# Two feed-forward networks behind a block-causal attention: one run for the eight wide down pieces of a step, another last visit, and an order for the scores

## The chip, the cores and the metric

One core of a Trainium2 chip runs the kernel. The metric is the device time of one execution in microseconds (us). A matmul runs on TensorE and writes PSUM; VectorE, ScalarE and GpSimd work elementwise beside it, GpSimd on SBUF alone; DMA queues are issued from SyncE (SP) and ScalarE.

## The reference

Attention over 4 batches of 8 heads, 576 positions and 64 values a head, then two feed-forward networks without a residual, on 2304 tokens of 512 values with 2048 hidden values:

```python
scores = q @ k.T / sqrt(64)                 # masked to block_i >= block_j, blocks of 64
attn = softmax(scores)                      # with 1e-9 in the denominator
x = (attn @ v)                              # to 2304 tokens x 512
h = x @ moe_w_in;  x = (h * sigmoid(h)) @ moe_w_out
h = x @ moe2_w_in; x = (h * sigmoid(1.702 * h)) @ moe2_w_out
```

## The kernel before

**Planning.** The kernel doesn't issue instructions in the order of its text. Each operation is handed to `Flow.add` (line 45) with its engine, an estimated duration, what it reads and writes, and a due time `at`. `Flow.run` (line 89) then simulates the engines: whenever one is free it issues the ready operation with the smallest due time. The order on each engine's queue is what comes out of this. The planner knows PSUM by banks; the waits that the program really gets are made from tiles. Banks 0 and 1 are one tile, `s8` (shown as `s` in the trace), the others have one each.

**Attention** works on 16 pairs of heads. Scores of a pair are 9 bands of rows (`AT`, line 456, says in which bank each lies), computed in three parts, `s_mm` 0, 1 and 2 (line 475 in the trace): part 0 holds bands 6, 7 and the tail of 8, part 1 holds 8, 5 and 1, part 2 the four small ones. Bands 8 and 6 lie in `s8`. `s_max` takes the row maxima on VectorE (line 485), `s_exp` the exponentials on ScalarE (line 495), `t_mm` transposes (line 549), `t_cp` copies them to SBUF (lines 408, 409), `o_mm` multiplies by the values (line 593) and `x_out` writes into `xy`, which holds all tokens. `plan` gives each of these a due time, `p * TAU + when`, and `HEAD` replaces it for the first two pairs.

**The networks** use a fast matrix scheme: a token block of 768 columns (`W`) is cut into two halves of 384, and seven up products (lines 724 to 726, six matmuls of 384 columns each, 128-row operands split into a high and a low part) give a pair of hidden blocks. `keep` (line 733) copies products 1 and 2 out of PSUM on ScalarE as c11 and c22, `comb` (line 738) adds the others on VectorE, and `hidden` (lines 752 to 754) makes the activation in two parts: two activations on ScalarE and a subtraction on VectorE. Products alternate between the two banks of `UB`. Hidden blocks live in three buffers, `g0` to `g2`. The down projection (lines 791 to 793) of a hidden block is cut into pieces (i, m, big): i is which of the two hidden blocks, m which 128 output rows, and big says whether it is the first 512 columns of the token block, or the last 256. A piece is three matmuls.

**Steps and visits.** A visit (l, z, p0, p1) takes token block z of layer l through weight pairs p0 to p1; its results add up in PSUM. A step is one pair: its seven up products, and between them the 16 down pieces of the step before. `SEQ` (line 843) is the pattern (M an up product, D a piece), `ORDER` (line 841) the order of the pieces, `LAST` that of the pieces behind the last step; a chain of edges keeps TensorE in this order. There are 48 steps. At a visit's end `evac` (line 805) copies PSUM out: a whole visit (`"all"`) straight to `xy`; a visit of half the pairs puts its part into DRAM (`"first"`), and `"last"` fetches it again and adds. The weights are brought from 64-bit data to two 32-bit parts by `w_scale` to `w_put` on ScalarE, VectorE and GpSimd, spread by the strings `SUM_ON` to `Y_ON` (p GpSimd, d VectorE), with earliest times in `EARLY`.

Of the kernel before, what the change touches and what calls it, by code (L numbers as in the profile page):

```python
# [134 lines left out]
def act(n):  # L135
    return 0.06 + n * 0.833e-3


def dve(n):
    return 0.06 + n / 960  # L140
# [18 lines left out]
def block_causal_attention_two_ffn(  # L159
# [9 lines left out]
    nc = tc.nc  # L169
    PSUM = bass.MemoryType.PSUM  # L170

    NP, P, S = qT.shape
    BLK = 64
# [7 lines left out]
    H = 256  # L181
    A, B = slice(0, BLK), slice(BLK, P)
# [7 lines left out]
    NWF = 8  # L190
    NSR = 6
    DIRECT = "1e11111100010101"
    VISITS = [(0, 0, 0, 4), (0, 1, 0, 8), (0, 2, 0, 8), (0, 0, 4, 8), (1, 1, 0, 4), (1, 2, 0, 8), (1, 0, 0, 8), (1, 1, 4, 8)]
    EARLY = [6.4, 47.4, 34.1, 18.5, 68.3, 94.6, 93.9, 120.4, 40.0, 36.9, 88.0, 0.0]
    SUM_ON = "dpdddppdpddddpdppdddppdpdpddddddppddppddddpdpppddppddppppdppppdp"
    COMB_ON = "ppdpddpddddpddddddddpddpddppddppddppppdpdddddpppdpdpdddppdppppdd"
    LOW_ON = "pppdpdddpddpdpdpdpddpddddpdpdpdddddpddpdddpdddddppdpdpdpdppppdppppdpppdpddpdpppddpddppdpppdpppddppdddpdppddppddpdppdpppdpppdpdpdppddpddddppdddpp"
    X_ON = "pdddpppp"
    Y_ON = "pppdppdddppppp"
    NWARM = 3  # L200
    TAU = 66.730
    LEADS = [90.0, 82.0, 24.0, 80.0]
    BEFORE = 1e4

# [1 line left out]
    add = flow.add  # L206
# [21 lines left out]
    bank = {i: T("psum", [P, 512], F32, f"bank{i}") for i in range(2, 8)}  # L228
# [4 lines left out]
    xy = T("cst", [P, ND, NT], F32, "xy")  # L233
# [4 lines left out]
    def xkeys(m, c0, n):  # L238
        return [("xy", m, i) for i in range(c0 // H, (c0 + n - 1) // H + 1)]
# [151 lines left out]
    def op(eng, us, fn, reads=(), writes=(), lag=0.0, size=0, sb=False, mode=0):  # L391
        x = add(eng, us, fn, reads, writes, clock[0] - BEFORE, lag=lag, size=size, name=tag[0], sb=sb, mode=mode)
        for k in [*reads, *writes]:
            ends["a2" if k[0] in ("q", "k", "pj") else "a3"].append(x)
        return x
# [54 lines left out]
    PIECES = [[0], [0, 1], [1]]  # L450
# [5 lines left out]
    def swapped(j):  # L456
        return j in SIDES[1]
# [8 lines left out]
    def s_mm(p, part):  # L466
        (q, kq), (k, kk) = src(p, "q"), src(p, "k")
        keys = sorted({("B", AT[j][0] + (AT[j][1] + c) // 512) for _, *blocks in ROUNDS[part] for j, c in blocks})

        def mms():  # L470
            for n, *blocks in ROUNDS[part]:
                for j, c in blocks:
                    for h, r in enumerate((A, B)):
                        t = s_out(j)[B if h != swapped(j) else A, c:c + n]
                        nc.tensor.matmul(t, q[r, j * BLK:(j + 1) * BLK], k[r, c:c + n], start=True, stop=True)  # L475

        us = sum(max(n * 4 / 2400, 0.117) for n, *_ in ROUNDS[part]) + 0.02
        op("pe", us, mms, [(*kq, i) for i in PIECES[part]] + [kk], keys, lag=0.25, mode=1)

    def mx_(p, j):  # L480
        return buf(p, f"mx{j}", [P, 1])

    def s_max(p, *js):
        for j in js:
            op("dve", dve((j + 1) * BLK) + 0.01, lambda j=j: nc.vector.tensor_reduce(  # L485
                out=mx_(p, j), in_=s_view(j), axis=AX.X, op=ALU.max, negate=True), s_keys(j) + [kpj(p, 6)] * (j == 8), [("mx", p % 2, j)])

    exps = {}
# [110 lines left out]
    def x_out(p, odd):  # L599
# [5 lines left out]


    plan = [
        (0, 2882.13, load, "q"), (0, 2559.47, load, "k"), (0, 2853.51, load, "v"), (0, 2905.64, q_scale),
        (0, 2571.85, s_mm, 0), (0, 2852.24, s_max, 6), (0, 2571.21, s_max, 7), (0, 2553.46, s_exp, 6), (0, 2574.72, s_exp, 7),
        (0, 2909.22, s_mm, 1), (0, 2548.52, s_max, 8), (0, 2859.72, s_max, 5, 1), (0, 2571.07, s_exp, 8), (0, 2571.14, s_exp, 5, 1),  # L610
        (1, 2528.21, r_add), (1, 2578.60, r_inv),
        (1, 2548.41, t_mm, 4), (1, 2546.87, t_cp, 4, "act"), (1, 2539.51, t_mm, 5), (1, 2953.00, t_cp, 5, "dve"), (1, 2543.63, t_mm, 2), (1, 2880.99, t_cp, 2, "act"),
        (1, 2573.39, t_mm, 6), (1, 2559.80, r_copy, "act"), (1, 2951.06, t_cp, 6, "dve"), (1, 2571.01, r_put), (1, 2848.29, r_get),
        (0, 2528.64, s_mm, 2), (0, 2853.46, s_max, 3, 2), (0, 2550.49, s_max, 4, 0), (0, 2543.88, s_exp, 3, 2), (0, 2544.58, s_exp, 4, 0),
        (0, 2864.95, t_mm, 3), (0, 2674.64, t_cp, 3, "act"), (0, 2560.07, t_mm, 0), (0, 2823.46, t_cp, 0, "act"), (0, 2537.30, t_mm, 1), (0, 2541.48, t_cp, 1, "dve"),
        (1, 2859.78, o_mm, 0), (1, 2906.59, x_out, 0), (1, 2541.65, o_mm, 1), (1, 2542.10, x_out, 1),
    ]
    HEAD = [
        [1331.35, 1183.59, 1237.43, 1178.46, 1181.21, 1177.07, 1237.42, 1338.75, 1233.62, 1208.86, 1178.82, 1171.94, 1336.59, 1186.67, 1185.06, 1336.24, 1194.98, 1335.90, 1324.40, 1175.47, 1181.33, 1218.37, 1322.23, 1167.71, 1186.69, 1323.52, 1218.49, 1181.33, 1325.54, 1178.91, 1324.53, 1196.09, 1175.99, 1323.28, 1327.08, 1198.04, 1194.56, 1189.76, 1217.91, 1179.86, 1175.67, 1188.66],
        [1225.77, 1102.38, 1243.55, 1132.89, 1117.25, 1261.59, 1247.55, 1083.79, 1246.56, 1245.30, 1264.82, 1261.35, 1250.56, 1160.55, 1223.04, 1245.52, 1201.93, 1121.74, 1217.49, 1248.42, 1264.66, 1239.58, 1158.04, 1143.68, 1217.77, 1152.81, 1245.54, 1151.65, 1132.78, 1267.65, 1245.33, 1142.47, 1064.30, 1245.04, 1241.74, 1148.17, 1130.98, 1249.77, 1102.40, 1135.54, 1251.23, 1201.93],  # L620
    ]

    def attention():
# [177 lines left out]
    def evac(l, z, m, big, part, t):  # L801
        c0 = z * W + (0 if big else 2 * H)
        t -= LEADS[3]
        if big:
            src, dst, keys, bk = bank[YB[m]], xy[:, m, c0:c0 + 2 * H], xkeys(m, c0, 2 * H), YB[m]
            rest = yd[l][:, m, :2 * H]
        else:
            src = bank[ZB[m // 2]].rearrange("p (a c) -> p a c", c=H)
            dst, keys, bk = xy[:, m:m + 2, c0:c0 + H], xkeys(m, c0, H) + xkeys(m + 1, c0, H), ZB[m // 2]
            rest = yd[l][:, m:m + 2, 2 * H:]  # L810
        ky = ("yd", l, m, big)
        x = nys[0] % 4
        ks = [("su", x, 0), ("su", x, 1)]
        nys[0] += part != "all"

        def st():
            y = f32(T("l3", [P, 2, 2 * P], F32R, f"su{x}"))
            return y.rearrange("p a c -> p (a c)") if big else y

        if part == "last":  # L820
            add("sp", 0.4, lambda: nc.sync.dma_start(out=st(), in_=rest), [ky], ks, t - 40, size=P * 2 * H * 4, after=gate("l3"))
            add("dve", dves(2 * H), lambda: nc.vector.tensor_add(dst, st(), src),  # L822
                [("B", bk), *ks], keys, t)
        else:
            o, w = (dst, keys) if part == "all" else (None, ks)
            if m % 2 == 0 and big:
                add("act", acts(2 * H), lambda: nc.scalar.copy(st() if o is None else o, src), [("B", bk)], w, t, after=gate("l3"))
            else:
                add("dve", dves(2 * H), lambda: nc.vector.tensor_copy(st() if o is None else o, src), [("B", bk)], w, t,
                    after=gate("l3"))  # L830
            if part == "first":
                add("sp", 0.4, lambda: nc.sync.dma_start(out=rest, in_=st()), ks, [ky], t, size=P * 2 * H * 4)
        if l == 1 and part != "first":
            for i in range(1 if big else 2):
                c = slice(c0, c0 + (2 * H if big else H))
                e, dma = ("act", nc.scalar) if part == "last" and m % 2 + i == 1 else ("sp", nc.sync)
                add(e, 0.4, lambda i=i, c=c, dma=dma: dma.dma_start(out=out[(m + i) * P:(m + i + 1) * P, c], in_=xy[:, m + i, c]),
                    xkeys(m + i, c.start, c.stop - c.start), [("out", m + i, c.start)], t, size=P * (c.stop - c.start) * 4)

    GROUPS = [(m, True) for m in range(4)] + [(m, False) for m in range(4)]  # L840
    ORDER = [(i, m, big) for i in range(2) for m, big in GROUPS]
    LAST = [(i, m, big) for m, big in GROUPS[4:] + GROUPS[:4] for i in range(2)]
    SEQ = "MDDDDMMDDDDMMDDDDMMDDDD"

    def feed_forward(t):
        pre = T("cst", [P, 1], F32, "pre")
        add("act", 1.5, lambda: nc.scalar.activation(pre, scale, AF.Silu), ["scale"], ["pre"], t - 60, after=list(exps.values()))
        U, D = 6 * mm(HALF), {True: 3 * mm(2 * H), False: 3 * mm(H)}
        steps = [(x, pr) for x in VISITS for pr in range(x[2], x[3])]
        done, got = set(), 0  # L850
# [108 lines left out]
```

## Time and profile before

| | us |
|---|---|
| median of 3 runs | 922.65 (922.56 to 923.07) |
| the profiled execution | 922.6 |
| its span, first to last instruction | 920.8 |
| TensorE busy | 905.4 |
| VectorE busy | 701.3 |
| ScalarE busy | 481.2 |
| GpSimd busy | 243.0 |

Matmuls are pipelined, so the duration of one in the trace is longer than the distance to the next. What a matmul costs in a stream is read from the starts: the start of one to the start of the next, called pitch below. A line of the timeline with x1 is one instruction, with x36 it is 36 merged into one; the name in brackets is what ended the engine's idle time in front of it.

### The profile page before, as it was taken

Reading aid. Unit: us, or ns where it says so; the run is one execution under the profiler, and the core shown is the slowest. Engines: PE = TensorE matmul, PEld = TensorE weight load, DVE = VectorE, ACT = ScalarE, POOL = GpSimd, SP = SyncE. Lnnn points to the kernel's source line nnn. Section 1 sums busy time; section 2 is a strip of 40 time slices with the busy share of each in tenths; the row PEclk is TensorE's granted clock in tenths of the full one; section 3 lists DMA queues with packets and bytes.
Section 4 is the critical chain, followed back from the end, with each engine's and each line's share of the span. In section 5 each row is a group of like instructions: output and inputs, shape, how many; then the busy total and the mean of one; then the engine's idle time right before and its main releaser. Section 6 shows DMA issues by size and latency. Waiting matters only on the chain.

```text
span 920.8 us, 17934 instructions
## 1 busy us (share of the span) xinstructions
PE 905.4 (98%) x6278; PEld 816.8 (89%) x6278; DVE 701.3 (76%) x1322; ACT 481.2 (52%) x1184; POOL 243.0 (26%) x237
## 2 busy tenths in 40 slices
PE   8999999999999999999999999999999999999997
PEld 5767777999999999999999999999999999999996
DVE  5898999998998988887796889896865734346534
ACT  6878987665455563544553645644545423235331
POOL 2224561224034333331242243423412200002000
PEclk9999999999999999999999999999999999999999
DMA  5455675988975696999977779699855766555722
GB/s 180 145 170 166 192 247 186 324 270 285 308 263 215 239 321 205 342 361 317 324 264 243 243 238 329 222 315 367 285 204 186 217 210 186 183 184 185 252 88 93
DMA packets 97066, 219.89 MB, mean 239 GB/s; under 512 B 11344, under 2 KB 15184, under 8 KB 96976
## 3 DMA queue, kind: packets, MB, share of 16 engines
q1 hardware_dynamic: 96400, 217.96, 71.2%
q8 instruction: 50, 0.82, 0.4%
q10 hardware_dynamic: 576, 0.79, 0.2%
q14 instruction: 40, 0.33, 0.1%
HBM read 164.63 MB, written 54.08 MB: 238 GB/s over the span
## 4 chain that ended last, share of the span: by engine, by line
PE 92%; ACT 2%; issue 2%; DVE 2%; DMA 2%; POOL 0%; SPq 0%; ACTq 0%; DVEq 0%; POOLq 0%
PE bank L724 13%; PE bank L726 13%; PE bank L725 13%; PE bank L792 10%; PE bank L793 10%; PE bank L791 10%; PE s L793 5%; PE s L792 5%; PE s L791 5%; PE bank L593 4%; PE bank L549 3%; PE s L475 2%; ACT p L495 2%; DMA v<-vP 1%; DVE mx L485 1%
## 5 line engine op out<-in xcount | busy, mean ns | idle before, releaser
L738 DVE TENSOR_TENSOR c<-c,bank 128x384 f32<-128x384 f32 x238 | 131.4, 552 | 129.5 <-PE bank L726 112.7
L724 PE MATMUL bank<-xc,wu 128*128 128x384 f32 x666 | 224.4, 337 | 0.0
L726 PE MATMUL bank<-xc,wu 128*128 128x384 f32 x666 | 224.0, 336 | 0.0
L725 PE MATMUL bank<-xc,wu 128*128 128x384 f32 x666 | 223.5, 336 | 0.0
L752 ACT ACTIVATE th<-c 128x384 f32<-128x384 f32 x192 | 100.3, 522 | 163.7 <-DVE c L738 162.6
L793 PE MATMUL bank<-g,wd 128*128 128x256 f32 (+1 forms) x576 | 183.5, 319 | 0.0
L792 PE MATMUL bank<-g,wd 128*128 128x256 f32 (+1 forms) x576 | 183.5, 319 | 0.0
L791 PE MATMUL bank<-g,wd 128*128 128x256 f32 (+1 forms) x576 | 182.7, 317 | 0.0
L754 DVE TENSOR_TENSOR g<-th,g 128x384 fp32r<-128x384 f32 x192 | 119.4, 625 | 29.0 <-ACT g L753 28.3
L724 PEld LDWEIGHTS bank<-xc,wu 128*128 128x128 f32 x666 | 125.5, 189 | 3.7
L725 PEld LDWEIGHTS bank<-xc,wu 128*128 128x128 f32 x666 | 125.5, 188 | 3.7
L726 PEld LDWEIGHTS bank<-xc,wu 128*128 128x128 f32 x666 | 125.0, 188 | 0.0
L792 PEld LDWEIGHTS bank<-g,wd 128*128 128x128 f32 x576 | 108.7, 189 | 8.7
L791 PEld LDWEIGHTS bank<-g,wd 128*128 128x128 f32 x576 | 108.6, 189 | 8.3
L793 PEld LDWEIGHTS bank<-g,wd 128*128 128x128 f32 x576 | 109.0, 189 | 7.7
L733 ACT COPY c<-bank 128x384 f32<-128x384 f32 x95 | 45.1, 475 | 127.9 <-PE bank L726 127.3
L753 ACT ACTIVATE g<-c 128x384 fp32r<-128x384 f32 x192 | 97.9, 510 | 0.0
L738 DVE TENSOR_TENSOR c<-c,c 128x384 f32<-128x384 f32 x96 | 66.6, 694 | 18.9 <-ACT c L733 17.2
L317 POOL TENSOR_TENSOR wf<-wf,wt 128x512 f32<-128x512 f32 x30 | 41.8, 1394 | 138.8 <-DVE wt L309 127.3
L793 PE MATMUL s<-g,wd 128*128 128x512 f32 x192 | 76.2, 397 | 0.0
L792 PE MATMUL s<-g,wd 128*128 128x512 f32 x192 | 75.9, 395 | 0.0
L791 PE MATMUL s<-g,wd 128*128 128x512 f32 x192 | 74.7, 389 | 0.8 <-DVE xy L822 0.8
(102 smaller groups left out, 1398.8 us busy)
## 6 DMA issues: line engine op xcount, KB each, us to landing
wu<-wk SPq DMA_DIRECT2D x266, 256.0 KB, 3.7
wd<-wk SPq DMA_DIRECT2D x74, 512.0 KB, 5.1
raw<-w SPq DMA_DIRECT2D x64, 512.0 KB, 5.8
wk<-wu SPq DMA_DIRECT2D x77, 256.0 KB, 3.7
wk<-wd SPq DMA_DIRECT2D x22, 512.0 KB, 4.2
wk<-su SPq DMA_DIRECT2D x35, 256.0 KB, 5.9
v<-vP SPq DMA_DIRECT2D x16, 320.0 KB, 2.9
wk<-sd SPq DMA_DIRECT2D x10, 512.0 KB, 6.1
```

The source lines that it names most:

```text
L317: op("pool", 1.42, lambda: nc.gpsimd.tensor_add(wf_(k), wf_(k), wt_(k)), [kw, kt], [kw], name=f"s.{k}")
L724: nc.tensor.matmul(o, w[:, 0, c], xc(u, 0, j), start=j == 0, stop=False)
L725: nc.tensor.matmul(o, w[:, 1, c], xc(u, 0, j), start=False, stop=False)
L726: nc.tensor.matmul(o, w[:, 0, c], xc(u, 1, j), start=False, stop=j == 1)
L733: add("act", acts(HALF), lambda: nc.scalar.copy(cb(o), bank[bk][:, :HALF]), [("B", bk)], [o], at - LEADS[3], after=gate(home(o)))
L738: add(e[0], e[1], lambda: e[2].tensor_add(cb(o), cb(x), bank[y][:, :HALF] if isinstance(y, int) else cb(y)), [x, yk], [o], at - LEADS[3], ...
L752: add("act", us, lambda: nc.scalar.activation(th(), cb(src), fn), [src], [k], at, after=gate(home(f"th{z}")))
L753: add("act", acts(HALF), lambda: nc.scalar.activation(gt(q + i, 0)[:, c], cb(src), fn), [src], [kg[0]], at, after=gate("l3"))
L754: add("dve", dves(HALF), lambda: nc.vector.tensor_sub(gt(q + i, 1)[:, c], th(), f32(gt(q + i, 0)[:, c])), [k, kg[0]], [kg[1]], at, after=g ...
L791: nc.tensor.matmul(o, w[:, 0, k], gt(q + i, 0)[:, c], start=st, stop=False)
L792: nc.tensor.matmul(o, w[:, 1, k], gt(q + i, 0)[:, c], start=False, stop=False)
L793: nc.tensor.matmul(o, w[:, 0, k], gt(q + i, 1)[:, c], start=False, stop=sp)
```

## The change

- `SEQ` and `ORDER`: the pieces of 256 columns of a step come first, four behind the third up product and four behind the fifth; all eight of 512 columns follow the seventh.
- `VISITS`: the last two visits change places, so that the last is a whole one, (1, 0, 0, 8). `LAST` has a new order for its 16 pieces.
- `evac`: for the block of the last visit in layer 1, each result of 512 columns is copied in two halves, on ScalarE and on VectorE, and each half is written out by its own DMA (SP and ScalarE queues).
- `s_mm`: part 1 of the scores is issued behind the maximum of band 6, and the exponential of band 6 behind part 1.
- All due times (`TAU`, `plan`, `HEAD`), `EARLY` and the strings that spread work over VectorE and GpSimd have other values. Of the first token block's split, 9 operations more are on VectorE (`X_ON` 3 to 7 d, `Y_ON` 4 to 9).

```diff
-    VISITS = [(0, 0, 0, 4), (0, 1, 0, 8), (0, 2, 0, 8), (0, 0, 4, 8), (1, 1, 0, 4), (1, 2, 0, 8), (1, 0, 0, 8), (1, 1, 4, 8)]
+    VISITS = [(0, 0, 0, 4), (0, 1, 0, 8), (0, 2, 0, 8), (0, 0, 4, 8), (1, 1, 0, 4), (1, 2, 0, 8), (1, 1, 4, 8), (1, 0, 0, 8)]
...
-    X_ON = "pdddpppp"
-    Y_ON = "pppdppdddppppp"
+    X_ON = "dddddddp"
+    Y_ON = "dpdpddpdddpdpd"
...
-    TAU = 66.730
+    TAU = 148.363
...
-        op("pe", us, mms, [(*kq, i) for i in PIECES[part]] + [kk], keys, lag=0.25, mode=1)
+        x = op("pe", us, mms, [(*kq, i) for i in PIECES[part]] + [kk], keys, lag=0.25, mode=1)
+        if part == 1:
+            for a, b in ((maxs[6], x), (x, exps[6])):
+                a.outs.append(b)
+                b.left += 1
...
+    maxs = {}
...
-            op("dve", dve((j + 1) * BLK) + 0.01, lambda j=j: nc.vector.tensor_reduce(
+            maxs[j] = op("dve", dve((j + 1) * BLK) + 0.01, lambda j=j: nc.vector.tensor_reduce(
...
+        if l == 1 and part == "all" and z == VISITS[-1][1]:
+            for i in range(2):
+                k, y = (m, c0 + i * H) if big else (m + i, c0)
+                o = xy[:, k, y:y + H]
+                x = bank[bk][:, i * H:(i + 1) * H]
+                e, us, fn, q = (("act", act(H), nc.scalar.copy, nc.sync), ("dve", dve(H), nc.vector.tensor_copy, nc.scalar))[i]
+                add(e, us, lambda o=o, x=x, fn=fn: fn(o, x), [("B", bk)], xkeys(k, y, H), t)
+                add("act" if i else "sp", 0.1 if i else 0.4, lambda o=o, k=k, y=y, q=q: q.dma_start(out=out[k * P:(k + 1) * P, y:y + H], in_=o),
+                    xkeys(k, y, H), [("out", k, y)], t + 1, size=P * H * 4)
+            return
...
-    ORDER = [(i, m, big) for i in range(2) for m, big in GROUPS]
-    LAST = [(i, m, big) for m, big in GROUPS[4:] + GROUPS[:4] for i in range(2)]
-    SEQ = "MDDDDMMDDDDMMDDDDMMDDDD"
+    ORDER = [(i, m, big) for big in (False, True) for i in range(2) for m in range(4)]
+    LAST = [(0, m, False) for m in range(4)] + [(0, m, True) for m in range(2)] + [(1, m, False) for m in range(4)]
+    LAST += [(1, 0, True), (1, 1, True), (0, 2, True), (1, 2, True), (0, 3, True), (1, 3, True)]
+    SEQ = "MMMDDDDMMDDDDMMDDDDDDDD"
```

In `plan`, the due times of one pair on TensorE were 2528.64 (scores part 2) to 2909.22 (part 1); now they are 3119.44 (part 1) to 3959.72 (first value product).

## Rows read from the trace of the kernel before

**Rows 1.** Page, part 1: busy us, share of the span, instructions

```profile
PE 905.4 (98%) x6278; PEld 816.8 (89%) x6278; DVE 701.3 (76%) x1322; ACT 481.2 (52%) x1184; POOL 243.0 (26%) x237
```

**Rows 2.** Stretch, PE, PEld, DVE, ACT, POOL busy us, granted clock, DMA share, GB/s

```profile
0.00:160.00 160.00, 149.67 (x1934) 111.55 (x1935) 136.30 (x316) 128.94 (x409) 55.09 (x72) 0.99 0.58 183
160.00:905.00 745.00, 745.00 (x4284) 696.17 (x4283) 558.47 (x997) 350.39 (x771) 187.90 (x165) 1.00 0.75 253
```

**Rows 3.** Timeline of TensorE, half a step: start us, duration us, line

```profile
301.17 0.34 PE L724 MATMUL bank<-xc,wu 128*128 128x384 f32 x1
...
303.25 0.39 PE L791 MATMUL s<-g,wd 128*128 128x512 f32 x1
...
305.33 0.39 PE L791 MATMUL bank<-g,wd 128*128 128x512 f32 x1
...
306.01 0.33 PE L724 MATMUL bank<-xc,wu 128*128 128x384 f32 x1
...
307.08 0.33 PE L724 MATMUL bank<-xc,wu 128*128 128x384 f32 x1
...
308.12 0.28 PE L791 MATMUL bank<-g,wd 128*128 128x256 f32 x1
...
309.55 0.34 PE L724 MATMUL bank<-xc,wu 128*128 128x384 f32 x1
```

**Rows 4.** Timeline of the last downs: TensorE, VectorE, last DMA issue

```profile
911.68 0.39 PE L793 MATMUL s<-g,wd 128*128 128x512 f32 x1
912.11 0.69 DVE L822 TENSOR_TENSOR xy<-su,s 128x512 f32<-128x512 f32 x1 [1.38 <-PE s L793]
912.85 0.50 PE L791 MATMUL s<-g,wd 128*128 128x512 f32 x1 [0.78 <-DVE xy L822]
...
913.43 0.39 PE L793 MATMUL s<-g,wd 128*128 128x512 f32 x1
...
916.16 0.39 PE L793 MATMUL bank<-g,wd 128*128 128x512 f32 x1
...
917.30 0.34 ACTq L837 DMA_DIRECT2D out<-xy  x1
```

**Rows 5.** Timeline of ScalarE: two copies c11, a prompt and a late one

```profile
295.12 0.48 ACT L733 COPY c<-bank 128x384 f32<-128x384 f32 x1 [0.48 <-PE bank L726]
...
608.48 0.68 ACT L288 ACTIVATE wf<-raw 128x512 f32<-128x512 f32 x1 [3.06 <-DMA raw<-w]
...
610.70 0.48 ACT L733 COPY c<-bank 128x384 f32<-128x384 f32 x1
```

**Rows 6.** Timeline: an operation on 256 columns of PSUM, on VectorE

```profile
103.36 0.42 DVE L603 TENSOR_TENSOR xy<-bank,rb 128x256 f32<-128x256 f32 x1
```

**Rows 7.** Timeline of the scores, pairs 0, 1 and a settled one

```profile
6.51 0.23 PE L475 MATMUL bank<-k,q 64*64 64x64 f32 x2
7.64 0.62 DVE L485 TENSOR_REDUCE mx<-s 128x1 f32<-128x448 f32 x1 [2.18 <-PE bank L475]
9.74 0.89 PE L475 MATMUL bank<-k,q 64*64 64x64 f32 x24 [2.04 <-ACT p L495]
17.77 0.76 DVE L485 TENSOR_REDUCE mx<-s 128x1 f32<-128x576 f32 x1 [0.49 <-ACT p L495]
101.03 0.63 ACT L495 ACTIVATE p<-s,mx 128x448 f32<-128x448 f32 x1 [0.37 <-PE bank L475]
```

**Rows 8.** Value products of attention, by the chain and by the timeline

```profile
44.47 2.96 PE bank L593 x36
54.44 2.96 PE bank L593 x36
147.85 2.94 PE bank L593 x36
92.78 2.94 PE L593 MATMUL bank<-pt,v 128*64 128x256 f32 x36 [0.71 <-ACT pt L408]
101.68 2.94 PE L593 MATMUL bank<-pt,v 128*64 128x256 f32 x36
```

More of the change, by code (lines that the diff above doesn't have):

```diff
@@ L192, in block_causal_attention_two_ffn @@
     DIRECT = "1e11111100010101"
-    VISITS = [(0, 0, 0, 4), (0, 1, 0, 8), (0, 2, 0, 8), (0, 0, 4, 8), (1, 1, 0, 4), (1, 2, 0, 8), (1, 0, 0, 8), (1, 1, 4, 8)]
[L194 to L197, printed above, removed]
-    X_ON = "pdddpppp"
-    Y_ON = "pppdppdddppppp"
+    VISITS = [(0, 0, 0, 4), (0, 1, 0, 8), (0, 2, 0, 8), (0, 0, 4, 8), (1, 1, 0, 4), (1, 2, 0, 8), (1, 1, 4, 8), (1, 0, 0, 8)]
+    EARLY = [2.3, 22.9, 38.0, 8.5, 0.6, 92.2, 4.2, 34.1, 64.0, 46.0, 134.1, 0.0]
+    SUM_ON = "pddpdpdpdddpdddddddppddddpddddddpdppddppddpppppdpdddddppdpppdddp"
+    COMB_ON = "dppdpdpppppdddddddddpdpddddpddppdppdddddpdppddddppddppdddpddpddp"
+    LOW_ON = "dpddppddpddpppddpddppddpdpddpdddddddpddpppdpddddpdddddpdddpddpdddpddppddpppddpdpdpdppdpppdppdpppppppdpdddpddddppddpdpddpppdppdddpdddddpdppppdppp"
+    X_ON = "dddddddp"
+    Y_ON = "dpdpddpdddpdpd"
     NWARM = 3
-    TAU = 66.730
+    TAU = 148.363
     LEADS = [90.0, 82.0, 24.0, 80.0]
@@ L607, in block_causal_attention_two_ffn @@
     plan = [
[L608 to L616, printed above, removed]
+        (0, 3138.06, load, "q"), (0, 3138.47, load, "k"), (0, 3411.46, load, "v"), (0, 3130.91, q_scale),
@@ new lines, in block_causal_attention_two_ffn @@
+        (0, 3411.04, s_mm, 0), (0, 3354.83, s_max, 6), (0, 3368.94, s_max, 7), (0, 3131.92, s_exp, 6), (0, 3177.91, s_exp, 7),
+        (0, 3119.44, s_mm, 1), (0, 3143.91, s_max, 8), (0, 3423.68, s_max, 5, 1), (0, 3180.49, s_exp, 8), (0, 3358.58, s_exp, 5, 1),
+        (1, 3964.99, r_add), (1, 3133.00, r_inv),
+        (1, 3387.68, t_mm, 4), (1, 3402.25, t_cp, 4, "act"), (1, 3123.78, t_mm, 5), (1, 3423.82, t_cp, 5, "dve"), (1, 3131.74, t_mm, 2), (1, 3154.97, t_cp, 2, "act"),
+        (1, 3140.82, t_mm, 6), (1, 3365.00, r_copy, "act"), (1, 3149.64, t_cp, 6, "dve"), (1, 3166.56, r_put), (1, 3353.44, r_get),
@@ L617, in block_causal_attention_two_ffn @@
+        (0, 3440.15, s_mm, 2), (0, 3967.29, s_max, 3, 2), (0, 3401.83, s_max, 4, 0), (0, 3401.94, s_exp, 3, 2), (0, 3353.69, s_exp, 4, 0),
+        (0, 3422.49, t_mm, 3), (0, 3445.41, t_cp, 3, "act"), (0, 3552.80, t_mm, 0), (0, 3374.94, t_cp, 0, "act"), (0, 3149.48, t_mm, 1), (0, 3136.25, t_cp, 1, "dve"),
+        (1, 3959.72, o_mm, 0), (1, 3175.63, x_out, 0), (1, 3420.50, o_mm, 1), (1, 3131.69, x_out, 1),
     ]
     HEAD = [
-        [1331.35, 1183.59, 1237.43, 1178.46, 1181.21, 1177.07, 1237.42, 1338.75, 1233.62, 1208.86, 1178.82, 1171.94, 1336.59, 1186.67, 1185.06, 1336.24, 1194.98, 1335.90, 1324.40, 1175.47, 1181.33, 1218.37, 1322.23, 1167.71, 1186.69, 1323.52, 1218.49, 1181.33, 1325.54, 1178.91, 1324.53, 1196.09, 1175.99, 1323.28, 1327.08, 1198.04, 1194.56, 1189.76, 1217.91, 1179.86, 1175.67, 1188.66],
@@ L620, in block_causal_attention_two_ffn @@
-        [1225.77, 1102.38, 1243.55, 1132.89, 1117.25, 1261.59, 1247.55, 1083.79, 1246.56, 1245.30, 1264.82, 1261.35, 1250.56, 1160.55, 1223.04, 1245.52, 1201.93, 1121.74, 1217.49, 1248.42, 1264.66, 1239.58, 1158.04, 1143.68, 1217.77, 1152.81, 1245.54, 1151.65, 1132.78, 1267.65, 1245.33, 1142.47, 1064.30, 1245.04, 1241.74, 1148.17, 1130.98, 1249.77, 1102.40, 1135.54, 1251.23, 1201.93],
+        [1091.39, 1103.64, 1183.82, 1087.64, 1101.42, 1097.96, 1130.47, 1098.52, 1127.30, 1120.58, 1104.14, 1120.40, 1123.14, 1104.14, 1114.21, 1122.40, 1117.26, 1183.70, 1089.20, 1125.63, 1122.26, 1063.21, 1119.80, 1089.16, 1070.27, 1100.75, 1091.03, 1093.26, 1117.07, 1113.10, 1124.15, 1090.70, 1118.48, 1119.06, 1099.66, 1117.96, 1095.97, 1102.17, 1084.36, 1133.18, 1104.23, 1094.68],
@@ L621, in block_causal_attention_two_ffn @@
+        [408.35, 398.20, 325.64, 325.15, 433.07, 343.11, 344.27, 381.00, 491.38, 382.15, 456.26, 345.83, 341.94, 409.28, 379.45, 380.92, 336.64, 382.47, 306.06, 490.08, 349.98, 334.25, 343.75, 339.08, 442.01, 436.23, 324.96, 491.21, 344.38, 343.60, 394.64, 340.29, 372.47, 441.21, 448.49, 316.32, 383.42, 328.64, 459.45, 438.29, 341.89, 328.34],
     ]
```

## The prediction

> **What bounds the kernel now.** I read the busy shares first [rows 1]: TensorE is busy 98% of the span, VectorE 76%, ScalarE 52%. A share is an average, so the table by stage comes next [rows 2]. Attention fills the first 160 us and TensorE has gaps there (149.7 busy of 160). From 160 to 905 us it is busy in all 745 us, with the other engines at 75%, 47% and 25%. Behind that stretch one wait is left, 0.78 us in the last downs [rows 4]. So the two networks are bound by the matmul stream itself: a faster ScalarE, VectorE or DMA gives nothing there, and only a shorter stream does, or a stall that is put into it. The granted clock is 1.00 throughout that stage [rows 2], the 2.4 GHz level.
>
> The stream then has to be read matmul by matmul [rows 3]. A step (one pair of weight blocks on one token block) is 42 matmuls of 384 columns, 24 of 512 and 24 of 256, and its runs last 2.08 (12 of 384), 2.76 (12 of 512), 2.11 (12 of 384) and 1.43 us (12 of 256), then comes a single up product of 1.04 us (six of 384, as from 307.08 to 308.12); with the second big, 384 and small run that is 2 x 2.76 + 2 x 2.11 + 2 x 1.43 + 2.08 + 1.04 = 15.72 us. Within a run the pitch isn't constant. The last three matmuls of the big run take 0.68 us, 0.227 each; the first nine take 2.08, where nine at 0.227 would take 2.04. The six up matmuls behind a big run take 1.07 us, the next six 1.04; and twelve take 2.11 behind a big run, 2.08 behind a small one. The runs shown stand for 94 big ones, 93 small ones and 94 and 93 of up matmuls behind them, whose lengths hardly vary. Measured against an even pitch (226.7, 173.3 and 120 ns), their means are +41 ns in a big run, +26 ns in the 384 run behind it, +7 ns in a 384 run behind a small one, and -13 ns in a small run.
>
> **The order of a step.** Before, the order is M, 4 big, MM, 4 small, MM, 4 big, MM, 4 small (M is six up matmuls, a piece three down matmuls). After, it is MMM, 4 small, MM, 4 small, MM, 8 big. No matmul is added or removed. Two entries into a big run and two exits become one of each. Per step the extras were 2 x (41 + 26 + 7 - 13) = 122 ns and become 41 + 26 + 2 x 7 - 2 x 13 = 55 ns: 67 ns less. There are 47 steps in which both kinds of work lie: **-3.15 us**. That a run of 24 has the entry cost once is borne out by the end of the kernel, where 12 matmuls in a row (913.43 to 916.16) take 2.73 us, 0.2275 each, well after the restart [rows 4]. Lower bound of the gain 0, if the extra returned every 12 matmuls; upper 47 x 0.12 = 5.7, if all of it went.
>
> The Trainium skill (TensorE: Matmul & The Clock Gate, section Back-to-back issue gap) gives a warm gap of N/2.4 + 2.5 ns, a function of the column count alone. By it the order would be worth nothing and this term would be 0 (forecast 921.05). The trace disagrees: 227 ns where the page's formula gives an estimate of 216, and a pitch that depends on the neighbours.
>
> **The third M in a row.** Up products alternate between two PSUM banks. Before, four pieces lie between any two products on one bank beside the other product; now the third M of the triple writes the bank of the first with only 1.04 us between. ScalarE's copy c11 must have emptied it. That copy takes 0.48 us [rows 5]. A prompt one, as at 295.12, starts 0.25 us after the next matmul's issue and ends 0.73 after it: 0.3 us to spare. The late one at 610.70 stands behind four activations, and these behind a weight scaling that had waited 3.06 us for DMA [rows 5]; it ends 1.9 us after the product, and in the new order TensorE would stand 0.9 us. Of the 47 copies of c11 before, 17 end more than 0.97 us after the product, together 4.4 us too late; but nearly all stand behind activations of the last two products, which the new order finishes 5.5 us earlier relative to the step's end. Of the 47 of c22, whose neighbours on ScalarE are like those of the new c11, two are late, by 0.03. Between 0 and +4.4 us I take **+0.6**, nearer to the c22 rows, with some room for scalings that wait for DMA. The hidden activations of the second block must now wait for the first four big pieces, whose operands they overwrite; they are then needed some 5 us later, and ScalarE and VectorE have 53% and 25% of their time free to catch up [rows 2]. I cost that at nothing; without the cover it lands in the same wait.
>
> **The last visit.** Before, the last downs make TensorE wait until 912.85: the two halves of tile s are banks 0 and 1, the copy of bank 0 waits for the matmuls into bank 1 (VectorE starts at 912.11, when the next group is done), and the next matmuls into bank 1 wait for that copy [rows 4]. In the new order both second pieces of these banks come before the copies, and the next four pieces go to other banks: 1.17 us between two issues (911.68, 912.85) becomes 0.23: **-0.94 us**. The new transitions among these pieces are worth +-0.06 by the means above.
>
> After the last matmul (issued 916.16, 0.39 long) the final sum on VectorE takes 0.69 us as at 912.11, the DMA is issued at 917.30 [rows 4] and the span ends at 920.8. New: a copy of 256 columns on ScalarE and one on VectorE, 0.42 each by the nearest row [rows 6], each with its own 128 KB DMA in place of one of 256 KB. If both copies ran at once this would give about -0.5. But two readers of one tile on different engines don't overlap here: the maximum at 17.77 us waits 0.49 us for ScalarE, which only reads that tile too [rows 7]. One behind the other they take about 0.85 plus a hand-over, 0.2 longer than now, against some 0.3 from the smaller DMA. I take **-0.1**, range -0.5 to +0.3. The Trainium skill (PSUM — Partial Sum Buffer, section PSUM bank collisions raise a hardware error) says that ScalarE and VectorE must not read one bank at once; the row agrees that they are kept apart. By the rule this term is the one that I take, without it -0.5 and the forecast 917.5. The new last visit is a whole block, so its partial sums aren't fetched at the end; those loads hid behind matmuls and are worth nothing.
>
> **Attention: the scores.** The change ties the order max 6, scores part 1, exponential 6. In pair 0, max 6 starts at 7.64 us, after waiting 2.18 us for TensorE; its own scores were done at 6.74, and it waited for part 1, which writes other columns of s [rows 7]. Starting 0.85 us earlier, it moves max 7, exponential 7 and with it part 2, for which TensorE stood idle 2.04 us until 9.74 [rows 7]: **-0.8 us**. In the settled pairs max 6 already comes before part 1, and exponential 6 already waits for part 1 (0.37 us at 101.03 [rows 7]): nothing changes there.
>
> **Attention: priorities and engines.** All due times are new, and 9 operations of the first token block's split go from GpSimd to VectorE. The twelve value products that start from 44.47 to 147.85 us lie 9.40 us apart on average; a good pair takes 8.90 (92.78 to 101.68), a bad one 9.97 (44.47 to 54.44) [rows 8]. What separates them is mostly the value product's wait for the last transposed copy (0.71 us at 92.78, one of eight such). So the new priorities can be worth from -5.5 (11 distances, 0.50 less each) to +7 us (12 pairs at 0.57 more). Their sign I can't read from rows; part 1 now has the smallest due time of a pair on TensorE and the first value product the largest, which puts other work between the two where the wait arises. I take **-0.3**.
>
> **Sum.** 922.6 (the profiled execution: span 920.8 and 1.8 around it; the median of the runs is 922.65) - 3.15 + 0.6 - 0.94 - 0.1 - 0.8 - 0.3 = 917.9, so **917.9**.
>
> **Rivals.** (a) Attention gains its whole slack: 917.9 - 5.2 = 912.7. For it: TensorE's waits there are few and of one kind. Against: VectorE is busy 85% there [rows 2] and gets more. (b) The order gives nothing, the extra returning with each four pieces: 921.05. Against: the 12 even matmuls at the end [rows 4]. (c) The copy of c11 comes as late as before: 917.9 + 3.8 = 921.7. (d) Slower: the new priorities let every pair end in the wait for the last transposed copy, and VectorE, with 9 more operations, feeds it late: 917.9 + 7.3 = 925.2. It turns the whole slower from 0.38 us more in each of the 12 pairs (4.6 us); below that the gains elsewhere cover it.
>
> **How the numbers follow.** Forecast 0.55 (its own range 915.5 to 920), (a) 0.18, (b) 0.08, (c) 0.09, (d) 0.10. Range 912 to 922: it takes in (a) to (c) but for half of (a)'s lower tail, and leaves out (d). A measurement of this kernel tells about 0.2%, 1.85 us, from no change: faster means below 920.8. Faster: the forecast, (a) and 0.03 of the best end of (b), 0.76; same: the rest of (b) and (c), 0.14; slower: (d), 0.10.
>
> **What would show it.** A step of 15.65 us in place of 15.72, with a run of 24 big matmuls in 5.48 us; no wait of TensorE on c11's copy in the list of waits (each entry there is rival c); no gap in the last downs; part 2 of pair 0 before 9 us; the first up product of the first step at or before 151 us. Wrong if value products lie over 9.5 us apart or matmuls of a triple M wait.

## The result, and the profile after

The changed kernel takes 913.91 us (median of four, 913.04 to 914.45) against 922.65: a ratio of 0.990, 95% interval 0.989 to 0.992. That is 4.0 us less than the 917.9 forecast: inside the range of 912 to 922, but outside the forecast's own range of 915.5 to 920, and nearer to rival (a) at 912.7. The profiled execution took 913.76, with a span of 911.9.

I cut the span at four events that both traces have: the first score matmul, the 43rd up matmul (the first step of the networks is done), the first matmul of the list `LAST`, and the last matmul's issue.

| stage, us | before | after | difference | forecast |
|---|---|---|---|---|
| start to first score | 5.64 | 6.39 | +0.75 | 0 |
| to the end of the first step (attention) | 162.43 | 157.01 | -5.42 | -1.1 |
| to the start of `LAST` (steps) | 738.83 | 736.52 | -2.31 | -2.55 |
| to the issue of the last matmul | 9.26 | 8.14 | -1.12 | -0.94 |
| to the end of the span | 4.64 | 3.88 | -0.76 | -0.1 |
| sum | 920.8 | 911.9 | -8.86 | -4.7 |

The steps came out near their forecast, attention and the tail did not. The start to the first score isn't the change's: it moves from one execution to the next (last section). The busy times by stretch answer to [rows 2] (stretch, PE, PEld, DVE, ACT, POOL busy, granted clock, DMA share, GB/s):

```profile
0.00:160.00 160.00, 156.29 (x1981) 114.96 (x1982) 138.71 (x329) 133.43 (x420) 51.35 (x69) 1.00 0.61 195
160.00:905.00 745.00, 744.72 (x4285) 697.86 (x4284) 559.59 (x1014) 354.57 (x765) 161.85 (x146) 1.00 0.74 251
```

TensorE has 3.7 us of gaps in the first 160 us, where it had 10.3. Which gaps went is in its list of waits (line waited for: us in total, times, longest). First the kernel before, then after:

```profile
PE bank L593 <- ACT pt L408: 5.5, 8, 0.7
PE bank L475 <- ACT p L495: 2.0, 1, 2.0
PE bank L628 <- DVE wt L627: 1.4, 1, 1.4
PE s L791 <- DVE xy L822: 0.8, 1, 0.8
PE s L475 <- DVE mx L485: 0.7, 3, 0.4
PE bank L549 <- ACT p L495: 0.2, 1, 0.2
```

```profile
PE bank L634 <- DVE wt L633: 1.4, 1, 1.4
PE bank L555 <- ACT p L501: 0.9, 3, 0.5
PE s L475 <- DVE mx L491: 0.7, 1, 0.7
PE bank L555 <- DVE pt L409: 0.3, 1, 0.3
PE bank L730 <- ACT c L739: 0.3, 1, 0.3
PE bank L475 <- ACT p L501: 0.2, 1, 0.2
```

All eight waits of the value product on ScalarE's copies are gone, 5.5 us, and nothing of that size stands in their place. Of the 2.0 of pair 0, 0.7 is left as a wait for max 6, and 0.2 in front of part 2. The 0.8 of the last downs is gone. One wait on c11 (line 739) is there, 0.3 us.

A step after, from TensorE's timeline (start, duration), answers to [rows 3]:

```profile
304.54 0.33 PE L730 MATMUL bank<-xc,wu 128*128 128x384 f32 x1
...
307.69 0.28 PE L797 MATMUL bank<-g,wd 128*128 128x256 f32 x1
...
314.72 0.39 PE L797 MATMUL s<-g,wd 128*128 128x512 f32 x1
...
316.80 0.39 PE L797 MATMUL bank<-g,wd 128*128 128x512 f32 x1
...
320.20 0.33 PE L730 MATMUL bank<-xc,wu 128*128 128x384 f32 x1
```

From 304.54 to 320.20 a step takes 15.66 us (15.72 before). The run of 24 takes 5.48; its last fifteen, from 316.80, take 3.40 or 0.2267 each, so that the entry is paid once. The other signs that the prediction named: the first up product of the first step starts at 147.31 (151.89 before), part 2 of pair 0 at 9.61, which is 3.22 after the first score (4.10 before), and of the matmuls of a triple M one waits.

The last downs and the end, which answer to [rows 4]:

```profile
908.06 0.39 PE L799 MATMUL bank<-g,wd 128*128 128x512 f32 x1
908.48 0.42 DVE L832 COPY xy<-bank 128x256 f32<-128x256 f32 x1 [0.94 <-PE bank L799]
908.94 0.37 ACT L832 COPY xy<-bank 128x256 f32<-128x256 f32 x1 [0.98 <-DVE xy L832]
908.95 0.34 ACTq L833 DMA_DIRECT2D out<-xy  x1
```

The two half copies don't overlap: ScalarE starts 0.04 us after VectorE has ended.

### The profile page after: what moved, and what is told of

Its sections match the earlier page's. It is cut to its first block, busy times and chain, and to the rows that moved or that the text cites. A ratio compares the mean times of both kernels' runs of the same rounds, so it can differ in the third digit from the quotient of the medians.

```text
span 911.9 us, 17882 instructions
## 1 busy us (share of the span) xinstructions
PE 904.5 (99%) x6278; PEld 815.3 (89%) x6278; DVE 700.0 (77%) x1346; ACT 489.7 (54%) x1188; POOL 213.2 (23%) x215
## 4 chain that ended last, share of the span: by engine, by line
PE 96%; ACT 1%; DMA 1%; DVE 1%; issue 0%; SPq 0%; DVEq 0%; ACTq 0%
PE bank L730 13%; PE bank L732 13%; PE bank L731 13%; PE bank L799 10%; PE bank L798 10%; PE bank L797 10%; PE s L799 5%; PE s L798 5%; PE s L797 5%; PE bank L599 5%; PE bank L555 5%; PE s L475 3%; PE bank L475 1%; ACT p L501 1%; DMA rb<-rd 1%; PE bank L634 1%
## 5 line engine op out<-in xcount | busy, mean ns | idle before, releaser
L759 ACT ACTIVATE g<-c 128x384 fp32r<-128x384 f32 x192 | 95.2, 513 | 24.7 <-PE bank L798 24.5
L744 DVE TENSOR_TENSOR c<-c,c 128x384 f32<-128x384 f32 x96 | 60.5, 630 | 16.5 <-ACT c L739 15.5
L317 POOL TENSOR_TENSOR wf<-wf,wt 128x512 f32<-128x512 f32 x25 | 34.9, 1396 | 136.4 <-DVE wt L309 108.0
```

The source lines that it names most:

```text
L744: add(e[0], e[1], lambda: e[2].tensor_add(cb(o), cb(x), bank[y][:, :HALF] if isinstance(y, int) else cb(y)), [x, yk], [o], at - LEADS[3], ...
L759: add("act", acts(HALF), lambda: nc.scalar.activation(gt(q + i, 0)[:, c], cb(src), fn), [src], [kg[0]], at, after=gate("l3"))
```

## The experiments

Stage times below are those of the table, in each kernel's own trace. "Attention" counts from the first score matmul, because its start moves by up to 1.2 us with the moment at which the clock rises (last section). The same attention differs between traces by 0.6: it takes 162.43 us in the kernel before and 163.01 with the order alone, 156.62 to 157.25 in the four kernels that have all of the changed one.

**The order alone, and the change without it.** Theory: the order is worth 67 ns a step by itself. Rival (c): c11 comes late and takes it back.

```diff
-    ORDER = [(i, m, big) for i in range(2) for m, big in GROUPS]
+    ORDER = [(i, m, big) for big in (False, True) for i in range(2) for m in range(4)]
-    SEQ = "MDDDDMMDDDDMMDDDDMMDDDD"
+    SEQ = "MMMDDDDMMDDDDMMDDDDDDDD"
```

The kernel before with this edit alone:

> The kernel before with the new order of the pieces within a step alone (SEQ, ORDER). If the cost of entering and leaving a big run is what the order saves: a step of 15.655 us in place of 15.72, big runs of 24 in 5.48 us, 47 x 0.067 = 3.1 us less, minus at most 0.6 of waits for the copy c11: 920.0. If the gain of the changed kernel in this stretch came from the other edits: 922.6. If c11's copy comes late as often as before: 921.5 or more.

The changed kernel with this edit undone:

> The changed kernel with the old order of the pieces within a step. If the parts add up: 913.9 + 2.3 to 2.6 = 916.4, with a step of 15.72 us and the ends of attention and of the last visit as in the changed kernel. If the order of the steps also made the gain elsewhere: 918 or more.

The order alone gives 923.67, ratio 1.000 (0.9995 to 1.0014): nothing. Its steps take 740.77 in place of 738.83, and the waits of that stage that the kernel before hasn't are these:

```profile
PE bank L726 <- DVE xc L679: 2.7, 2, 1.5
PE bank L724 <- ACT c L733: 1.1, 1, 1.1
```

2.7 us are waits for the halves of a token block (`xc`), which three up products in a row want sooner, and 1.1 is c11, rival (c). A wait costs its step more than the list has. By the starts of the first up product of each step, the steps of the kernel before take 15.72 us and those of this run 15.65, but for four that are longer by 4.9 in all (the three in which these waits lie, and the one behind the second) and two that are longer by 0.15. So 3.15 is gained, 5.1 is lost, and 1.9 more is left. The copy of c11 stands behind a weight scaling that waits for DMA, as the chain of waits shows:

```profile
606.68 6.73 DMA raw<-w
613.43 0.66 ACT wf L288
614.09 0.38 ACT c L733
614.51 0.44 PE bank L724
```

The changed kernel with the old order takes 916.41, ratio to before 0.993 (0.992 to 0.995). Its steps take 739.61; with the new order 736.52. So the order is worth 3.09 us there, and 2.5 by the medians of the whole. Step by step the gain is the 3.15 of the forecast (15.720 to 15.653 us, 47 times); a late c11 takes 0.55 of it back in one step, and in the second step, the first behind attention, 0.50 comes on top. With the old order this second step is 0.78 longer than in the kernel before, and all later ones take 15.72: that much the other edits cost the networks, which was in no term of the forecast. The same order is worth -3.1 in one plan and +1.9 in another.

**The tie in pair 0, alone.** The old plan's own order is kept instruction by instruction, and two of them are moved: part 1 of the scores behind max 6, and exponential 6 behind exponential 7, both in pair 0 only.

```diff
+        if p == 0 and part == 1:
+            flow.behind += [(x, maxs[0, 6]), (exps[6], exps[7])]
...
+        for a, b in self.behind:
+            seq.remove(a)
+            seq.insert(seq.index(b) + 1, a)
```

> The kernel before with its own instruction order, except in the first pair of heads: part 1 of the scores is issued behind the maximum of band 6, and the exponential of band 7 ahead of that of band 6. Theory A (the tie of scores part 1 to max 6 and the clock that falls in the idle time which it shortens make most of the gain in attention): part 2 starts near 8.9 us in place of 9.74, the granted clock in 10 to 15 us stays near 1.00 in place of 0.66, and the end of attention comes 2 to 2.6 us earlier: about 920.2. Theory B (the new due times make the gain, pair by pair; the tie is worth the 0.85 us of one wait): 921.8, and the clock dips as before. Theory C (the start is hidden by a later wait): 922.6.

TensorE's rows of pair 0 in it answer to [rows 7]:

```profile
7.93 0.54 PE L482 MATMUL s<-k,q 64*64 64x384 f32 x2 [0.71 <-DVE mx L496]
...
9.34 0.39 PE L482 MATMUL bank<-k,q 64*64 64x64 f32 x6 [0.21 <-ACT p L506]
```

Part 2 starts 3.22 us after the first score in place of 4.10: 0.88 sooner, as forecast (0.85). The value product of pair 1 is 1.5 us earlier, the end of the first step 0.7, hardly more than the 0.6 by which the same attention differs between traces. The granted clock in 10 to 15 us is 1.00, as theory A had it, but the time is that of theory B. The whole takes 921.92 against 922.48, ratio 0.9993 (0.9984 to 1.0003): the edit's own gain can't be told from none.

**The idle time of pair 0 filled.** The granted clock fell to its lower level behind that idle time (last section). To see what this costs, two matmuls whose result nobody reads are put into it; the order stays.

```diff
+            if p == 0 and part == 1:
+                for _ in range(2):
+                    nc.tensor.matmul(bank[4], wt_(0)[:, :P], wt_(0), start=True, stop=True)
```

> The kernel before with its own order, and two extra matmuls of zeros (their result is read by nobody) behind part 1 of the first pair's scores, in the 2.04 us in which TensorE stands idle; part 2 can't start earlier. Theory A: the clock doesn't fall behind the idle time, so the transposes and the 32 score matmuls that took 1.90 and 2.92 us at half clock take 1.0 and 2.05: 1 to 1.7 us less, 921.2. Theory B (the clock is not what costs there): 922.6, or a little more if the extra matmuls outlast the wait.

922.21 against 922.48, ratio 0.9996 (0.9987 to 1.0005). The clock doesn't fall, attention takes 161.39 in place of 162.43. That the filling kept the clock up isn't shown: it rose at 7.34 us in this trace, and kernels in which it rose that late kept it without filling too (last section). But a trace without the fall is only 1.0 us shorter in attention, so the fall costs about 1 us at most and isn't what attention gained.

**One part of the attention edits at a time.** Theory of the prediction: tie, due times and spread (`EARLY` and the strings) each bring a small, separate gain. Rival: they belong to one plan and mean nothing alone. Four runs put one part into the kernel before: the tie, as in the diff of the change;

> The kernel before with the tie alone (max 6, part 1, exponential 6 in each pair), all due times as before; the planner may order what follows differently. Theory A: end of the first step of the networks 2 to 3 us earlier than 168.07 us, about 920. Theory B: at most 0.85 us earlier, and not better than before if the old due times don't suit the tied order: 922 to 924.

`TAU`, `plan` and `HEAD`;

> The kernel before with the new due times of attention alone (TAU, plan, HEAD), without the tie. Theory B: end of the first step near 164.5 us in place of 168.07, value products below 9.2 us apart in place of 9.40: about 919. Theory A: without the tie the idle time and the slow clock of the first pair stay; end of the first step at 167 or later, 922 or more.

`EARLY` and all five strings;

> The kernel before with the new spread over VectorE and GpSimd and the new earliest times alone (EARLY and the five strings). If VectorE's load decides attention: end of the first step later than 168.07 by up to 2 us (9 operations more on VectorE): 924. If it is worth nothing in itself: within 0.7 us of 922.6. If it makes a part of the gain (fewer GpSimd operations in the way of VectorE): 1 to 2 us less.

and `X_ON` and `Y_ON` alone.

> The kernel before with the new strings X_ON and Y_ON alone, which move nine operations of the first token block's split from GpSimd to VectorE. The prediction counted that as a charge on VectorE in attention. If that charge is real, the value products lie 9.5 us apart or more and the first step ends after 168.5 (168.07 before); if those moves feed the first step earlier, it ends at 165 to 167.5; if they only matter through the planner's order, it ends anywhere from 160 to 180 with the order of attention changed as a whole.

Two take one part out of the changed kernel: the tie, and the new spread.

```diff
-        if part == 1:
-            for a, b in ((maxs[6], x), (x, exps[6])):
-                a.outs.append(b)
-                b.left += 1
```

> The changed kernel without the tie, all else as in it. Theory A: the first pair waits as before (part 2 at 9.7 us or later, granted clock in 10 to 15 us well below 1), end of the first step 2 to 3 us later than 163.4: 916 to 917. Theory B: 914 to 914.8.

```diff
-    EARLY = [2.3, 22.9, 38.0, 8.5, 0.6, 92.2, 4.2, 34.1, 64.0, 46.0, 134.1, 0.0]
+    EARLY = [6.4, 47.4, 34.1, 18.5, 68.3, 94.6, 93.9, 120.4, 40.0, 36.9, 88.0, 0.0]
...
-    X_ON = "dddddddp"
-    Y_ON = "dpdpddpdddpdpd"
+    X_ON = "pdddpppp"
+    Y_ON = "pppdppdddppppp"
```

> The changed kernel with the old EARLY and the old strings of engines (SUM_ON, COMB_ON, LOW_ON, X_ON, Y_ON); order, tie, due times and last visit are the changed kernel's. Two theories of the 4.7 us by which the first step ends earlier than forecast by 3.6. If the due times with the tie make it, the first step ends at 163 to 165 here, and what is lost lies behind it as waits on copies, 0 to 5 us as in the run of the new order with old strings. If due times and spread of the split belong together, the first step ends 5 or more us later than 163.4, as it did where only one of the two was new (178.25 and 176.37).

Attention in the traces, from the first score to the end of the first step; idle is the time in which no matmul of TensorE runs:

| kernel | whole, us | attention | of it idle |
|---|---|---|---|
| before | 922.65 | 162.43 | 8.90 |
| + tie | 981.24 | 214.41 | 35.35 |
| + due times | 933.95 | 171.40 | 10.34 |
| + spread | 931.84 | 169.52 | 9.84 |
| + `X_ON`, `Y_ON` | 930.42 | 168.16 | 9.14 |
| after, without the tie | 923.58 | 165.26 | 7.71 |
| after, with the old spread | 929.56 | 161.53 | 3.76 |
| after | 913.91 | 157.01 | 2.27 |

The kernel before took 922.48 to 923.35 beside these runs, each of which was made once. Each of the four parts put in alone makes it slower, by 7 to 59 us, and each of the two taken out alone loses 10 to 16. Of the expected times only the open ones were met (922 or more for the due times; a first step that ends between 160 and 180 us for `X_ON` and `Y_ON`). The planner's order of attention comes out new as a whole each time. With the tie alone TensorE waits all through attention for exponentials and copies:

```profile
PE bank L555 <- ACT p L501: 16.1, 15, 2.2
PE bank L555 <- DVE pt L409: 4.9, 7, 1.1
```

The run with the old spread stalls behind attention, at the third up product of a row: c11 is queued on ScalarE behind activations that wait 5.88 us for VectorE, which is busy with splitting weights and with the last results of attention (ScalarE, then TensorE):

```profile
175.53 0.52 ACT L758 ACTIVATE th<-c 128x384 f32<-128x384 f32 x1 [5.88 <-DVE g L760]
...
177.20 0.46 ACT L739 COPY c<-bank 128x384 f32<-128x384 f32 x1
```

```profile
177.71 0.69 PE L730 MATMUL bank<-xc,wu 128*128 128x384 f32 x1 [7.67 <-ACT c L739]
```

So the rival holds: what these parts gain, they gain together. The old spread was to end the first step at 163 to 165 us or 5 us later than 163.4; it ended at 167.79, between the two. Idle time isn't all of it: this run has 3.76 us, 5.1 less than the kernel before, and yet its attention is only 0.9 shorter. The same matmuls are busy 157.8 us in it, 154.7 in the changed kernel and 153.5 before; what lengthens them isn't shown. The run of `X_ON` and `Y_ON` was meant to show nine more operations on VectorE as a charge. It can't: the groups of value products are cut up anew, and the distances from pair 1 on are 9.58, 8.95 and 8.09 us before they become longer.

**The last visit.** The changed kernel with the old list and whole copies:

```diff
-    LAST = [(0, m, False) for m in range(4)] + [(0, m, True) for m in range(2)] + [(1, m, False) for m in range(4)]
-    LAST += [(1, 0, True), (1, 1, True), (0, 2, True), (1, 2, True), (0, 3, True), (1, 3, True)]
+    LAST = [(i, m, big) for m, big in GROUPS[4:] + GROUPS[:4] for i in range(2)]
```

> The changed kernel with its last visit as before: the list LAST with the two halves of a tile one behind the other, one copy of 512 columns for each piece and one DMA of 256 KB for it. All else is the changed kernel's. Theory of the prediction: the stall of about 0.8 us in the last downs comes back, so that the stretch from the start of the list LAST to the issue of the last matmul is 9.0 to 9.3 us in place of 8.14, and the end of the first step stays at 163.4 within 0.5. For the tail, from the last issue to the end of the span, 3.88 in the changed kernel: if the halved copies and DMAs made it 0.76 shorter than before, it is 4.5 to 4.8 here; if that was chance of the execution, it stays at 3.8 to 4.1. Sum about 915.5 to 916.

and with the new list, one copy of 512 columns, but two DMAs:

```diff
+            if m % 2 == 0 and big:
+                add("act", acts(2 * H), lambda: nc.scalar.copy(dst, src), [("B", bk)], keys, t)
+            else:
+                add("dve", dves(2 * H), lambda: nc.vector.tensor_copy(dst, src), [("B", bk)], keys, t)
...
-                add(e, us, lambda o=o, x=x, fn=fn: fn(o, x), [("B", bk)], xkeys(k, y, H), t)
```

> The changed kernel with one copy of 512 columns in place of two of 256 for each piece of the last visit, but still two DMAs of 128 KB, on SP's and ACT's queue. Tells what shortened the tail. If it is the size of the DMAs: the two copies behind one another (0.42 and 0.37) become one of about 0.65, and the tail from the last issue to the end of the span is 3.6 to 3.9. If the halved copies made it: 4.5 to 4.8. The list LAST is the changed kernel's, so the stretch from its start to the last issue stays at 8.1 within 0.2, and the end of the first step at 163.4 within 0.5.

They take 915.73 and 912.88 us. With the old list the wait is back (0.68 us, below) and the stretch takes 9.08 in place of 8.14: the list is worth 0.94.

```profile
905.77 0.59 ACT L833 COPY xy<-s 128x512 f32<-128x512 f32 x1 [6.95 <-PE s L799]
906.41 0.50 PE L797 MATMUL s<-g,wd 128*128 128x512 f32 x1 [0.68 <-ACT xy L833]
...
909.72 0.39 PE L799 MATMUL bank<-g,wd 128*128 128x512 f32 x1
910.15 0.69 DVE L835 COPY xy<-bank 128x512 f32<-128x512 f32 x1 [1.97 <-PE bank L799]
```

The tail is 4.20 us there, 4.08 with one copy and two DMAs, 3.88 with halves, and 4.64 in the kernel before; neither run fell into one of the brackets expected for it. Followed through SyncE's events of the end: the last DMA is issued 1.15 us after the last matmul with whole copies and 1.28 with halves; it lands 2.03 later with 256 KB, 1.75 with 128 KB issued alone. So halves and small DMAs together give 0.15. Another 0.17 comes from fewer semaphores that SyncE has still to look at after the landing (one in the changed kernel, three with the old list). The remaining 0.45 isn't the last visit's: with the same old end, five kernels (before, and those with the pair 0 order, the fill, the spread, the `X_ON` and `Y_ON`) have a tail of 4.63 to 4.66 and three (order, tie, due times) one of 4.19 or 4.20; the difference lies between SyncE's last drains. Each kernel has one trace, so whether this goes with the program or with the execution stays open.

The run with one copy is 0.16 us under the fastest of the changed kernel's four, with a first score 0.66 earlier in its trace; this is no better version.

## Why the prediction was right in its range, and where its steps were off

The gain is 8.7 us where 4.7 was forecast. The range held because rival (a) was taken into it; the terms of the networks were right, and attention and the tail gave the rest.

- **The order, -3.15.** Right: 3.09 by the run with the old order, a step of 15.65 us, a run of 24 in 5.48. The Trainium skill (TensorE: Matmul & The Clock Gate, section Back-to-back issue gap) gives the warm gap by the column count alone, in a formula that it calls that of an isolated matmul; of a stream it says that weight loads and matmuls set the spacing together. By a gap that hangs on the column count alone, moving pieces would be worth nothing; the step, 15.65 in place of 15.72 us, decides against that here.
- **The third M, +0.6.** Right in size: one of 47 copies makes TensorE wait, and its step takes 0.55 longer. The cover that I named (copies come sooner because activations do) shows in the run of the order alone too: of the 17 late copies one still makes TensorE wait, 1.1. What I didn't see is the wait for the halves of the next block, 2.7 there; it is the plan of the changed kernel that takes it away. That the stage came so near its forecast (-2.31 for -2.55) is luck in part: the 0.27 that the second step takes longer than the others was in no term.
- **The last downs, -0.94.** Right: 0.94 by the run with the old list.
- **The tail, -0.1.** Right as to what was costed: copies one behind the other, the DMA 0.28 shorter, together -0.15. The Trainium skill (PSUM — Partial Sum Buffer, section PSUM bank collisions raise a hardware error) says that ScalarE and VectorE must not read one bank at the same time; that ScalarE starts at 908.94, when VectorE has ended, agrees. The missing 0.6 lies behind the landing, where I costed nothing, and 0.45 of it can't be put down to the change.
- **The tie, -0.8.** Right at its place (0.88), wrong as a term of the sum: alone it gives about 0.7 by the end of the first step and nothing that can be measured at the end, and in the planner's hands, alone, it costs 59 us.
- **Due times and spread, -0.3, and of the settled pairs "nothing changes there".** This is the step that failed: the waits of the value products for the last transposed copy were taken to stay nearly whole; they went, and attention gained 5.42. What happened is rival (a), which had 0.18: behind pair 1's value product TensorE's idle time fell from 5.77 us to 0.07. In front of it the fall was 0.93. Against these 6.63 stand 1.21 more of busy time for the same matmuls, though the clock no longer falls in pair 0. The transposes of the settled pairs got longer, 137 ns busy for each against 130 (from the groups by line: busy us, mean ns, idle time before them; before, then after):

```profile
L549 PE MATMUL bank<-ident,p 128*128 128x128 f32 x300 | 39.0, 280 | 0.0
L593 PE MATMUL bank<-pt,v 128*64 128x64 f32 (+4 forms) x433 | 35.7, 318 | 5.5 <-ACT pt L408 5.5
```

```profile
L555 PE MATMUL bank<-ident,p 128*128 128x128 f32 x306 | 41.9, 281 | 0.1
L599 PE MATMUL bank<-pt,v 128*64 128x64 f32 (+4 forms) x432 | 35.7, 318 | 0.0
```

Why the wait could go is seen one queue further back, where I had not looked. ScalarE's timeline, with two rows of TensorE, ahead of the value product at 92.78 [rows 8], before:

```profile
87.87 2.30 PE L549 MATMUL bank<-ident,p 128*128 128x128 f32 x18
...
89.57 0.70 ACT L495 ACTIVATE p<-bank,mx 128x512 f32<-128x512 f32 x1
...
91.02 0.28 PE L475 MATMUL s<-k,q 64*64 64x128 f32 x2
...
91.39 0.63 ACT L495 ACTIVATE p<-s,mx 128x448 f32<-128x448 f32 x1 [1.03 <-issue]
...
92.16 1.05 ACT L408 COPY pt<-bank 128x512 f32<-128x512 f32 x2
```

and in the changed kernel, ahead of one at 107.08:

```profile
105.14 0.70 ACT L501 ACTIVATE p<-bank,mx 128x512 f32<-128x512 f32 x1
...
106.09 0.58 ACT L408 COPY pt<-bank 128x512 f32<-128x512 f32 x1
106.57 0.62 ACT L501 ACTIVATE p<-s,mx 128x448 f32<-128x448 f32 x1
...
107.08 0.49 PE L599 MATMUL bank<-pt,v 128*64 128x320 f32 x2
```

Before, exponential 6 (448 columns) stands in ScalarE's queue ahead of the last two transposed copies and waits 1.03 us there, while the transposes were done by 90.2. The profile names no releaser ("issue"); by the times it starts when the matmuls of part 1 that write the same tile are through, at 91.3. Eight exponentials 6 wait like this, 0.84 to 1.11 us, four of them with line 475 of TensorE named as releaser; two copies stand behind each of them, and behind these the eight value products that wait. In the changed kernel, from the pair at 43 us on, exponential 6 never waits: the copies go ahead of it, or the value product comes 1.8 to 1.9 us later. I had the 0.37 us of this wait in a good pair [rows 7] and took it as a sign that nothing changes; it was the same wait that in the bad pairs made the value product late. With the tie the planner knows that exponential 6 can't start before part 1, and can put copies into that time. But the tie isn't what took the wait away. In the lists of waits, the value product's wait for copies stands wherever the old due times are (5.5 us before, 3.7 with the tie, 3.8 with the spread, 4.0 with `X_ON` and `Y_ON`) and is gone wherever the new ones are, with or without tie and new spread: not one in the changed kernel without the tie, none with the old spread, and one with the due times alone:

```profile
PE bank L593 <- ACT pt L408: 0.2, 1, 0.2
```

So the new due times end this wait, and tie and spread are needed because without them other waits, or longer matmuls, come in its place. That it is the order of copies and exponential 6 by which the due times do it is argued from the two orders and not shown by a run: one that moves only the last copies of the old order ahead of exponential 6 was not made.

The lower bound of this term, -5.5 from the good and bad pairs of the old plan, held: the gain went to that end, and not to the value near the middle that I took. But the sign by which I had worked it out, the distance of the value products, doesn't show the gain: from pair 2 to pair 13 they lie 9.36 us apart, 9.40 before. 44 matmuls of scores and 6 transposes that stood ahead of pair 1's value product now stand behind it and fill the time that was idle, and the value products come sooner as a whole.

## What to carry to other kernels

Where a wait recurs on the engine that bounds a stage, follow it one queue further: the copy it waits for may be prompt but queued behind an instruction that waits for something else, and then a different order can take all of these waits away at once. Values of a list scheduler (due times, edges, engine strings) are one setting; put in one at a time each cost 7 to 59 us here, and together they gained 5.4 in attention, so a forecast shouldn't add them up as separate terms. The pitch of matmuls depends on their neighbours, 3.1 us here from grouping equal widths, and it only shows where the new order doesn't bring waits that take it back (5.1 us with the order alone).

## What the runs showed of the hardware

The clock at the start varies between executions: it rises at 4.36 to 7.55 us into the span, and the first score lies at 5.64 to 6.85, in four of the 14 traces ahead of the rise. The same idle time of 2.04 us on TensorE in pair 0 has the granted clock fall to 0.50 (1.2 GHz) afterwards in some traces and not in others. The stretch behind it, in the kernel before and in the changed kernel without the tie (the third number from the right is the granted clock, 0.57 and 1.00):

```profile
11.00:15.00 4.00, 3.80 (x30) 2.08 (x32) 2.07 (x6) 2.51 (x11) 1.39 (x2) 0.57 0.48 163
```

```profile
11.00:15.00 4.00, 3.63 (x59) 2.50 (x48) 2.97 (x8) 3.84 (x16) 0.70 (x3) 1.00 0.50 166
```

It fell in the three kernels with this idle time whose clock had risen by 5.38 us, and not in the three where it rose at 5.58 or later; whether the moment of the rise decides it isn't shown. In the run with the old spread the clock fell in the wait of 7.67 us too, and TensorE was busy again before it came back (granted clock 0.61, 0.50 and 0.61):

```profile
172.00:176.00 4.00, 0.00 (x0) 0.00 (x0) 3.97 (x9) 0.47 (x2) 0.00 (x0) 0.61 1.05 404
176.00:180.00 4.00, 2.29 (x7) 2.29 (x8) 1.58 (x3) 1.66 (x5) 0.00 (x0) 0.50 0.96 313
180.00:184.00 4.00, 4.00 (x20) 4.00 (x20) 0.61 (x2) 0.48 (x1) 0.00 (x0) 0.61 0.13 52
```
